# A new global order and engine choice for the 1444 operations of a fused long-convolution and gated-MLP kernel

## The chip, the cores and the metric

The kernel runs on one core of a Trainium2 chip. The core has five engines with a queue of instructions each: TensorE (PE in the profile; its weight loads are shown apart as PEld), VectorE (DVE), ScalarE (ACT), GpSimd (POOL) and SyncE (SP), whose queue here issues nearly all DMAs. The metric is the device time of one execution in microseconds; lower is better. A kernel's time is the median of several runs.

## What is computed

The inputs are 2048 tokens of 640 channels in bfloat16. Cut to what matters, the reference is this:

```python
mod = (silu(c) @ w_mod).reshape(1, 6, 1, 640)      # sa, ca, ga, sb, cb, gb
h = layernorm(q) * (1 + ca) + sa
# block A: a causal convolution of 4 taps, then one as long as the sequence
k_shift = sum(k_pad[:, t:t+S, :] * shift_k[:, 3-t] for t in range(4))
kv = k_shift * v
y = irfft(rfft(kv, 4096) * rfft(ssm_k, 4096))[:2048] + kv * ssm_D
x = q + ga * (h * y)
# block B: a gated MLP with a product over the sequence, Fh = 864
h = layernorm(x) * (1 + cb) + sb
z = gelu(h @ w_in)                                 # 2048 x 1728
z1, z2 = z[..., :864], layernorm(z[..., 864:])
g = w_sp @ z2 + b_sp[:, None]                      # w_sp is 2048 x 2048
out = x + gb * ((z1 * g) @ w_out)
```

## The kernel before

**How work is recorded and ordered.** The kernel does not issue instructions as it goes through its loops. Each step is recorded in a list, the class `Plan` (lines 119 to 154): `op(eng, kind, fn, ...)` stores which engines may do the step (`eng`, a string out of P, A, D, G, S for TensorE, ScalarE, VectorE, GpSimd, SyncE), a name (`kind`), the function that issues it, the tiles and parts of tiles that it reads and writes, and the tiles that it allocates. From these come its dependencies. There are 1444 steps; a step may be one instruction or many (the one called `taps` or `zz` issues up to ten and more matmuls). Then `Plan.run` (line 143) walks through the string `ORDER` (lines 47 to 114). A token of it such as `P1290` says: now issue step 1290, on TensorE. So this one string sets three things at once: the order in which each engine's queue is filled, the engine of every step that may go to more than one, and the order in which the tiles of a rotating pool are handed out. Between engines nothing but the dependencies sets the order. An engine does its queue strictly in order: where its next step has to wait, all behind it wait too.

**Steps 0 to 764, the convolution.** The 640 channels are cut into 5 slices of 128. For each slice u, `taps` multiplies K by diagonal weight matrices on TensorE (line 605), VectorE multiplies the result by V (`tv`, line 612), and the long convolution follows as three steps of matrix products: a first small transform (`s1`, copied out of PSUM by `s1c`), the forward transform with the tables M2 (`fwd`), for the filter and for the data, copies of the filter's half (`khc`, on ACT mostly), the complex product (`prod`, line 495, on VectorE), whose halves are summed by `csum` (line 505, GpSimd or VectorE), the inverse transform with the tables G2 (`inv`), casts of its result (`zc`, lines 278 and 514 on, ACT or VectorE), a transposing DMA (`zt`), and a last small transform (`y`). GpSimd and VectorE share the rest: the modulated h (`xn`, line 692; `ghm`, line 748, a multiplication by 1 + ca and an addition of sa), the gate and the residual (`ym`, `res`, line 808). The last slice has no time for a DMA, so TensorE transposes it (`zfl`, `zk`, `yl`, `yml`).

**The passage, steps 765 to 820 about.** The second layer norm of the first 512 tokens (`ag2`, `rstd2`, `nmr2`, `zx`), done in pieces as the last slice's columns come in; TensorE transposes each piece (`hfl`, line 971), VectorE and ACT modulate it (`hmod`, line 978; step 777 is one of those on VectorE). Step 1042 is one of four fillers (`fill`, lines 1062 to 1067): two matmuls of `ident` with itself, whose result nobody reads; it allocates a PSUM tile of the tag `s1`, which `hfl` uses as well.

**The MLP's first product, `zz` (line 1024).** 64 steps in 4 groups of 512 tokens, ten or so matmuls each step, GELU on ACT out of PSUM, statistics on VectorE (`stz`, line 1040), normalisation (`zn`, line 1052). Groups 1 to 3 are transposed by DMA (`turn`) and modulated by `hmod2`.

**The product over the sequence, steps 1045 to 1270.** The 16 row blocks of `w_sp` are taken in 8 pairs p = 0 to 7 (block p and block p + 8), and each pair's four products by the two halves of z2 are done with seven in Strassen's manner: `product(p, m)` (line 1115), m = 1 to 7, eight matmuls each. Their operands are sums of weight blocks, `ssum` (line 1096, VectorE or GpSimd, four for each pair), and sums of z2 blocks made once (`tsum`). The results are combined in SBUF by `keep`, `c11`, `partial`, `c22`, and by the closing pair `lsa` (line 1166) and `lsm` (line 1168, VectorE or GpSimd), which adds the bias and multiplies by z1. Two tiles u per pair (block p and block p + 8) then go through a transposing DMA, `turnu` (line 1173), into tiles uT. Steps 1137 and 1147, for example, are products of pair 1; the DMAs of its two blocks are 1142 and 1150.

**The projection, steps 1271 to 1443.** Pairs 0 and 7 are projected plainly (`pp`, line 1348). Pairs 1 to 6 use seven products again (`pq`, `piece`, line 1335): `usum` (line 1326, VectorE or GpSimd) makes four sums R of uT blocks for each pair, `vsum` makes those of the weights once; `ok`, `os`, `ox`, `oa` combine results, `pa` (line 1394) closes them with the residual, and a DMA writes each block of 128 tokens (`out`). Steps 1290 and 1292 are the first two `pq` of pair 1: 1290 needs the uT of block 1, 1292 the first sum R, which needs the uT of block 9. Step 1427 is the last `pq` of pair 6, 1430 the first `pp` of pair 7's first block. The weights of a pair are loaded by transposing DMAs (`ldwt`), 6 tiles in turn; there are 4 tiles uT.

**What sets the order in the old `ORDER`.** Per engine the string holds 407 steps for TensorE, 481 for VectorE, 272 for ScalarE, 189 for GpSimd and 95 for SyncE. In the spatial product TensorE runs, for each pair, products first and projections some six to eight steps behind: after product 1137 come six products and three `pp` before 1290, after 1147 three products and two `pq` before 1292.

## Time and profile before

| | |
|---|---|
| three runs | 305.51, 306.11, 307.37 us |
| median | 306.11 us |
| profiled execution, by its span | 303.8 us |
| DMA packets, bytes, mean rate | 117155, 41.57 MB, 137 GB/s |
| VectorE, busy | 260.4 us in 527 instructions |
| ScalarE, busy | 164.0 us in 299 instructions |
| GpSimd, busy | 186.8 us in 213 instructions |

The profile is one execution. Its span runs from the first instruction to the last; the runs' times hold what lies around it too. Busy time counts the instructions that compute; the issue of a DMA, a branch or a wait does not count. Matmuls overlap in their pipeline, so a TensorE that is busy throughout need not run at its peak, but it has no time in which it waits for anything. A row of the view by windows gives, for one stretch of time, each engine's busy time with the count of its instructions in brackets, the TensorE clock that the throttle granted as a share of full speed, the mean number of busy sixteenths of the DMA engines as a share, and the rate. A row of the view by groups gives the line of the code, the engine, the operation, output and input by the names of their tiles, and the sum and the mean duration of one; after the bar stands the idle time of the engine just before those instructions, and what ended it. In rows of the timeline the first column is the start in microseconds, the second the duration of all instructions of the row together.

### The profile page before, as it was taken

Reading aid. Unit: us, or ns where it says so; the run is one execution under the profiler, and the core shown is the slowest. Engines: PE = TensorE matmul, PEld = TensorE weight load, DVE = VectorE, ACT = ScalarE, POOL = GpSimd, SP = SyncE. Lnnn points to the kernel's source line nnn. Section 1 sums busy time; section 2 is a strip of 40 time slices with the busy share of each in tenths; the row PEclk is TensorE's granted clock in tenths of the full one; section 3 lists DMA queues with packets and bytes.
Section 4 is the critical chain, followed back from the end, with each engine's and each line's share of the span. In section 5 each row is a group of like instructions: output and inputs, shape, how many; then the busy total and the mean of one; then the engine's idle time right before and its main releaser. Section 6 shows DMA issues by size and latency. Waiting matters only on the chain.

```text
span 303.8 us, 7152 instructions
## 1 busy us (share of the span) xinstructions
PE 293.1 (96%) x2827; PEld 207.0 (68%) x2827; DVE 260.4 (86%) x527; ACT 164.0 (54%) x299; POOL 186.8 (61%) x213
## 2 busy tenths in 40 slices
PE   6899999999999999799999999999999999999996
PEld 2788999999989988645555555555555555665664
DVE  8899999999989999989595988988678798886794
ACT  5989999998888865446665779500111102111110
POOL 5463788839769997577537342099531863476771
PEclk9999999999999999869999999999999999999999
DMA  7999869792397978005997900057654446452433
GB/s 143 270 242 271 194 177 282 134 223 39 77 186 163 287 122 276 2 2 105 157 234 154 197 0 4 0 117 150 132 133 90 102 112 141 102 84 73 91 83 121
DMA packets 117155, 41.57 MB, mean 137 GB/s; under 512 B 102557, under 2 KB 117122, under 8 KB 117122
## 3 DMA queue, kind: packets, MB, share of 16 engines
q1 hardware_dynamic: 116968, 41.08, 62.0%
q8 instruction: 22, 0.36, 0.5%
q14 instruction: 11, 0.09, 0.1%
q10 hardware_dynamic: 154, 0.05, 0.1%
HBM read 16.60 MB, written 2.63 MB: 63 GB/s over the span
## 4 chain that ended last, share of the span: by engine, by line
PE 80%; DVE 8%; SPq 5%; DMA 3%; issue 2%; POOL 1%; ACT 0%; DVEq 0%; POOLq 0%
PE ps L1126 23%; PE pu L275 19%; PE pz L275 17%; PE po L1335 5%; PE sm L275 5%; PE s L275 4%; SPq L570 3%; DVE Tf L495 3%; PE po L1348 3%; DMA ZT<-in_A_v_dram 3%; PE pz L1126 2%; PE pu L1126 1%; DVE Z L616 1%; SPq L585 1%; DVE ot L1394 1%
## 5 line engine op out<-in xcount | busy, mean ns | idle before, releaser
L275 PEld LDWEIGHTS <-Z 128*128 128x128 bf16 x320 | 32.0, 100 | 28.8 <-issue 3.0
L275 PE MATMUL pu<-X,M 128*128 128x128 bf16 (+1 forms) x480 | 45.6, 237 | 0.9 <-DVE Tf L495 0.7
L509 POOL TENSOR_TENSOR W<-Tf 128x256 bf16<-128x256 f32 x42 | 30.7, 745 | 15.0 <-DVE Tf L495 9.0
L275 PEld LDWEIGHTS <-M 128*128 128x128 bf16 x480 | 36.7, 98 | 4.2 <-issue 1.6
L1126 PEld LDWEIGHTS <-S 128*128 128x128 bf16 x256 | 25.0, 98 | 20.8
L275 PE MATMUL pu<-big,Z 128*128 128x432 bf16 x160 | 34.6, 360 | 0.0
L278 ACT CAST X<-s 128x1024 bf16<-128x1024 f32 x32 | 32.7, 1021 | 3.3 <-PE s L275 3.2
L275 PE MATMUL pz<-big,Z 128*128 128x432 bf16 x160 | 33.0, 349 | 0.0
L495 DVE TENSOR_TENSOR Tf<-pu,KH 128x1024 f32<-128x1024 f32 x25 | 30.3, 1215 | 1.2 <-ACT Z L278 0.5
L1132 ACT COPY m<-ps 128x432 f32<-128x432 f32 x7 | 3.6, 521 | 49.8 <-PE ps L1126 41.0
L1126 PEld LDWEIGHTS <-wT 128*128 128x128 bf16 x192 | 18.8, 98 | 15.3
L278 ACT CAST Z<-pz 128x512 bf16<-128x512 f32 x40 | 23.5, 596 | 4.9 <-PE pz L275 4.7
L275 PEld LDWEIGHTS <-G 128*128 128x128 bf16 x330 | 24.6, 98 | 1.8 <-issue 0.4
L278 ACT CAST KH<-pu 128x512 bf16<-128x512 f32 x40 | 23.1, 592 | 3.8 <-PE pu L275 3.4
L1126 PE MATMUL ps<-X,wT 128*128 128x432 bf16 x112 | 22.7, 346 | 0.0
L1126 PE MATMUL ps<-X,S 128*128 128x432 bf16 x112 | 22.6, 346 | 0.0
L1040 DVE BATCH_NORM_STATS2 stz<-X 128x6 f32<-128x432 bf16 x32 | 18.1, 588 | 5.0 <-ACT X L1034 4.9
L1126 PE MATMUL ps<-T,S 128*128 128x432 bf16 x112 | 22.2, 346 | 0.0
L275 PE MATMUL sm<-dg,big 128*128 128x128 bf16 x320 | 20.7, 219 | 1.1 <-DVE Z L616 1.0
L275 PEld LDWEIGHTS <-big 128*128 128x128 bf16 x320 | 18.9, 98 | 2.0 <-issue 1.6
L495 DVE TENSOR_TENSOR T<-pu,KH 128x1024 bf16<-128x1024 f32 x15 | 18.2, 1215 | 1.9 <-PE pu L275 1.8
L275 PEld LDWEIGHTS <-X 128*128 128x128 bf16 x288 | 17.8, 98 | 2.2 <-POOL X L433 0.7
(223 smaller groups left out, 666.7 us busy)
## 6 DMA issues: line engine op xcount, KB each, us to landing
wm<-in_w_mod_dram SPq DMA_DIRECT2D x6, 800.0 KB, 4.9
xt<-in_A_q_dram SPq DMA_DIRECT2D x4, 640.0 KB, 5.6
out_dram<-ot SPq DMA_DIRECT2D x15, 160.0 KB, 1.9
big<-in_B_w_in_dram SPq DMA_DIRECT2D x2, 1080.0 KB, 7.8
X<-in_A_ssm_k_dram SPq DMA_DIRECT2D x4, 512.0 KB, 6.2
ZT<-in_A_v_dram SPq DMA_DIRECT2D x1, 1024.0 KB, 7.6
big<-in_A_v_dram SPq DMA_DIRECT2D x1, 1024.0 KB, 7.8
w_o<-in_B_w_out_dram SPq DMA_DIRECT2D x6, 160.0 KB, 3.5
```

What stands on the lines that cost most here:

```text
L275: nc.tensor.matmul(o, lhsT=w, rhs=x, start=start, stop=stop)
L278: (e.copy if e is nc.scalar else e.tensor_copy)(dst, src)
L495: e.tensor_tensor(T_[:], (tl[pu] if src is None else tl[src])[:, :, :, None, :].to_broadcast(shape), tl[KH][:, :, None, :, :].to_broadcast ...
L509: e.tensor_tensor(tl[W][:, :, o, :], T_[:, :, 0, o, :], T_[:, :, 1, 1 - o, :], op=ALU.add if o else ALU.subtract)
L570: e.dma_start_transpose(k_of(u)[:, KPAD + h * m:KPAD + (h + 1) * m], A_k[0, h * m:(h + 1) * m, u * DU:(u + 1) * DU])
L585: e.dma_start(v_of(0, ns.start, NT // n) if u0 == 0 else tl[name][:], v_nat[:, ns, ds])
L616: e.tensor_tensor(dst, tl[ps][:].rearrange("p n (c g) -> p n c g", g=8), v_of(u, i * SCH, SCH).rearrange("p n (c g) -> p n c g", g=8), op= ...
L1040: op("D", "stz", lambda e, i=i, n=n, fc=fc: e.bn_stats(out=stz[:, n, fc, :], in_=tl[z2][:, i, fc * FC:(fc + 1) * FC]), r=[(z2, (i, fc))], ...
L1126: nc.tensor.matmul(ps[:, :FC], lhsT=lhs[:, s_, :], rhs=rhs(s_), start=(s_ == 0 and not more), stop=(s_ == HT - 1), skip_group_check=more)
L1132: e.copy(part[p, m][:], part[p, BANK[m]][:, :FC])
L1335: nc.tensor.matmul(ps[:, :HS], lhsT=w(k), rhs=x(k), start=start and k == 0, stop=stop and k == n - 1, skip_group_check=True)
L1348: e.matmul(po[t, i][:, :hi - lo], lhsT=uTs[t][:fsz[ft], ft, :], rhs=T["w_o"][:fsz[ft], ft, lo:hi], start=(ft == 0), stop=(ft == NFT - 1))
```

## The change

Only the string `ORDER` is replaced: 68 lines by 70. No step is added, removed or altered; the same 1444 steps are issued, with the same dependencies and tile pools. What differs is the sequence, and the engine of about 130 steps that may go to more than one. By kind, old engine to new:

| steps | moved |
|---|---|
| `ghm` | 9 VectorE to GpSimd, 11 GpSimd to VectorE |
| `zc` | 5 ScalarE to VectorE |
| `zn` | 6 ScalarE to VectorE, 4 VectorE to ScalarE |
| `csum` | 6 VectorE to GpSimd, 5 GpSimd to VectorE |
| `ssum` | 6 GpSimd to VectorE, 2 VectorE to GpSimd |
| `usum` | 8 GpSimd to VectorE, 4 VectorE to GpSimd |
| `lsm` | 5 GpSimd to VectorE, 1 VectorE to GpSimd |
| the rest | single ones of `xn`, `zx`, `zk`, `s1c`, `hmod2`, `res`, `oa`, `c22`, `gbm`, tables |

VectorE's queue holds 502 steps after it (481 before), GpSimd's 173 (189), ScalarE's 267 (272); TensorE's 407 and SyncE's 95 stay, in another sequence. The lines of the string that hold the steps named above, old and new:

```diff
 ORDER = """
...
-D510 P519 A520 P529 S588 P688 P523 G511 A530 D512 D689 P690 P513 D691 A524 A514 D639 P692 D693 P724 P728 D725 A729 P694
...
-D767 G719 D768 D740 D706 G723 D741 G769 P751 D770 D742 D743 G771 A772 D700 P773 D699 D780 D745 P774 D775 D776 D777 G701
-A778 D721 D746 D781 A779 G676 G782 S598 D759 P1042 D748 D749 D704 D703 D702 G677 D783 D645 P793 D752 D760 D845 G784
...
-G1091 P1133 G1092 D1107 D1139 P1143 A1134 D1095 G1108 D1271 S1097 P1135 D1144 D1145 P1137 S1096 G1113 D1136 G1146 P1147
-S1088 P1158 P1283 D1140 P1281 D1141 D1111 S1100 G1110 S1142 D1282 D1148 P1151 D1109 P1153 D1149 A1152 D1284 P1155 S1099
-D1159 P1163 P1276 D1112 D1164 A1154 G1272 P1290 P1157 D1156 P1167 S1150 D1286 S1101 P1171 P1178 P1278 A1172 D1287 P1295
-D1274 D1160 S1285 D1165 A1291 D1273 D1115 D1296 D1161 D1114 D1277 P1175 P1173 D1168 D1288 A1174 P1292 P1183 P1302 P1177
...
-G1419 P1420 S1270 D1417 D1421 D1423 S1405 P1424 P1427 D1428 P1430 G1418 S1429 D1425 D1431 P1432 S1426 P1435 D1433 P1438
...
+P521 D522 P497 A498 P509 D510 P519 A520 G527 G528 P529 A530 S687 P688 D689 P523 G511 G512 D647 A524 P690 D691 D676
...
+D745 P758 D759 P1042 P751 G771 A772 P773 D775 D776 D780 D777 D781 G677 P774 A779 S765 A778 P796 P793 A797 D752 D746
...
+D1092 G1068 S1088 P1276 D1095 D1277 S1098 P1133 P1143 A1134 D1108 S1097 D1273 D1139 D1144 P1135 D1136 P1137 G1110
+D1140 D1141 P1278 D1279 S1096 P1281 D1145 D1111 P1147 D1148 G1146 D1149 P1151 S1142 P1290 A1291 D1282 P1153 D1272
+A1152 D1109 P1302 D1303 P1158 S1150 D1286 P1292 D1287 D1274 P1295 D1112 D1114 D1288 D1296 S1280 S1099 P1283 P1163
...
+G1418 G1419 P1420 D1421 D1425 S1426 P1430 P1427 D1428 P1432 S1429 D1431 D1433 S1434 P1435 P1441 D1436 S1437 D1442
...
 """
```

Read along one letter, the lines give one engine's queue. After product 1137 TensorE's now holds 1278, 1281, 1147, 1151 and then 1290; after 1147 it holds 1151, 1290, 1153, 1302, 1158 and then 1292. In the passage the filler 1042 stands ahead of 751, the last table product of the last slice; 511 and 512, the last two sums of the complex product, are both GpSimd's (512 was VectorE's). On SyncE's queue the first loads come in another sequence; then a load of modulation weights (573) goes ahead of a transposing load of K columns (31), another transposing load of K columns (33) ahead of a filter load (97), the two loads of `w_in` (765, 766) change places, and the first loads of the weights of the product over the sequence (1045 to 1052) come in another sequence around `turn` 919.

More of the change, by code (lines that the diff above doesn't have):

```diff
@@ L108 @@
[L108 to L111 removed]
+G5 D13 D0 D14 D18 A1 P7 D10 S2 P1044 G110 G109 D111 D112 G6 P8 P1043 A4 A16 G15 D17 A11 S83 S84 D113 D19 D90 D118 G89
@@ new lines @@
+P257 A258 A553 D65 P277 D278 G279 P100 A101 P315 A316 G105 P273 G559 D549 D270 D554 G555 P227 D228 P201 A202 S35 P66
+D67 G280 S579 P580 P283 D581 P591 A592 D274 P333 A334 D556 G565 S36 A564 D284 D569 D566 G570 G571 P271 A272 P72 A567
+P339 D73 P287 D288 A340 P293 D294 P70 P68 D71 D289 P329 A330 P383 A384 D572 P321 G74 G568 A322 P281 D282 P299 D300
+P337 S593 S594 G290 A560 D37 D600 P331 A338 A332 P285 A286 P303 D304 G604 P335 A336 P291 A292 D69 P323 A324 G295 P275
+D606 D623 D296 P317 A318 S595 D605 D607 P385 D660 D601 A386 P327 P297 A276 A328 G602 D603 D679 P341 D342 P389 A390
@@ new lines @@
+D631 P425 D426 A360 P435 P371 A372 P632 D633 P463 A464 P349 P634 P465 D723 A466 D436 D635 G683 S107 P481 A482 A350
+P421 P419 A420 P405 A406 P636 D422 D637 D638 D618 P483 A484 P397 A398 G617 P423 D424 D641 P477 A478 P487 P469 A488
+A470 P431 G427 G428 P429 A430 D663 D432 G437 G720 G438 P439 P441 D442 P485 A486 P451 S582 D452 P583 D640 P473 A474
+A440 A584 S666 D684 G620 P433 G659 P667 P471 A434 P479 G643 A472 D668 P669 D639 A480 G443 G444 P445 A446 D670 D642
+P489 D490 G453 G454 G717 G491 D645 P449 G682 A450 P671 D672 G492 P467 A468 P505 D506 P455 A456 P673 D674 G675 P475
@@ new lines @@
+G782 D644 D783 A784 D704 D749 D702 D750 G785 D747 P825 P787 A791 G648 S598 A794 D646 A826 P786 D845 D705 D748 D846
+D753 D844 D843 G847 D760 D764 D754 P827 A828 A792 D848 D849 G851 A852 G850 D788 S853 P823 P800 A801 P821 A822 D790
+A824 D789 P814 A815 G706 D619 D711 D649 D710 D653 D656 D678 D714 P829 A830 A140 D715 D652 D654 S599 S1046 P807 P831
+D707 D761 A832 S1045 P803 D651 A804 D757 P835 A836 P833 A857 A834 A808 D854 D855 P810 A811 D709 D713 P817 A818 G856
+D858 D655 P895 A896 D756 D911 D708 D755 D912 D650 D910 D909 G913 D805 P880 P893 A894 P859 A881 P901 A902 P862 D657
@@ new lines @@
+D879 D937 D886 D931 D865 P1012 D872 G903 D951 D952 D799 G837 D904 D941 D907 A992 G1057 G1059 D838 D1054 D1055 S1049
+D906 D934 D938 P994 A1013 A995 G1053 D945 G969 A840 P998 S1051 A999 D1000 P965 D1010 A966 P1015 A1016 D1017 D908 A842
+P963 A964 A841 P1001 P1019 A1020 A1002 P953 A954 P1031 D1007 A1032 D1011 D993 D970 D905 P961 A962 D839 A971 D1070
+D1003 G1056 P1023 D1014 D972 D1018 D1004 D996 D997 D1069 P1029 G1035 A1030 A1024 P1027 A974 P1021 A1022 D1036 P1025
+A1026 D1038 D1039 P1033 P1077 A1028 A1040 D1060 A1034 A1078 D973 D1037 D1071 D1072 D1075 D1073 D1074 D1058 P1079 A1080
@@ new lines @@
+D1169 G1298 D1305 P1178 P1171 D1294 D1297 D1301 S1162 P1314 A1315 A1172 S1170 D1310 D1311 S1101 G1313 D1116 D1179
+D1117 P1307 P1173 P1316 D1113 P1319 D1299 D1308 A1174 D1320 A1317 G1323 G1318 P1326 P1177 P1175 D1180 P1191 S1102
+S1285 D1119 D1176 D1181 S1182 S1306 D1322 D1120 P1183 D1184 A1192 P1195 D1327 D1321 P1187 D1185 G1186 D1312 P1338
+S1309 D1188 D1189 S1190 P1324 D1325 A1339 P1328 D1122 D1196 P1350 P1331 D1332 D1118 D1329 G1334 D1351 S1104 P1198
+D1199 D1335 D1337 S1330 S1333 D1336 P1203 D1204 P1193 A1194 G1205 G1206 P1343 D1344 P1340 P1348 A1341 D1121 P1197
@@ new lines @@
+D1200 D1201 S1103 P1352 P1207 P1211 P1213 A1214 S1202 D1347 D1342 D1208 P1362 D1209 S1210 D1125 G1345 D1349 D1123
+P1355 D1346 S1106 D1353 S1354 D1356 D1358 D1359 P1218 A1212 P1215 D1219 D1216 P1364 A1365 D1366 P1217 D1220 D1221
+P1367 A1363 D1368 G1360 P1372 G1361 P1223 D1369 D1224 D1225 G1370 P1374 P1376 D1375 P1227 D1373 D1228 G1226 G1229
+D1377 S1105 S1357 S1222 S1230 P1386 A1387 P1379 P1233 D1124 D1126 P1398 D1382 D1383 D1384 P1238 P1231 G1371 D1380
+D1399 D1127 P1388 A1389 D1390 D1128 D1130 A1234 A1232 D1239 P1391 P1396 G1385 P1400 D1392 G1395 P1243 D1244 D1129
```

85 lines of the change are left out of this document (29 added, 56 removed).

## The prediction

> **What bounds the kernel now.** I read the page first: its span, its busy shares and the row of the granted clock.
>
> ```profile
> span 303.8 us, 7152 instructions
> ...
> PE 293.1 (96%) x2827; PEld 207.0 (68%) x2827; DVE 260.4 (86%) x527; ACT 164.0 (54%) x299; POOL 186.8 (61%) x213
> ...
> PEclk9999999999999999869999999999999999999999
> ```
>
> TensorE (PE) is busy for 293.1 of 303.8 us, and the clock falls in two slices out of 40, the 17th and 18th (121.5 to 136.7 us). Then I cut the span by stage: the long convolution (0 to 119), the passage into the gated MLP (119 to 134), its first product (to 190.8), its spatial product and projection (to 290), the tail.
>
> ```profile
> core 0: us, PE busy (x) PEld busy (x) DVE busy (x) ACT busy (x) POOL busy (x), PEclk, DMA share, GB/s
> 0.00:25.00 25.00, 21.31 (x240) 16.79 (x241) 21.69 (x65) 20.79 (x46) 13.24 (x35) 1.00 1.09 216
> 25.00:60.00 35.00, 34.71 (x541) 32.86 (x541) 33.11 (x61) 34.03 (x64) 25.02 (x34) 1.00 0.89 217
> 60.00:90.00 30.00, 29.95 (x425) 28.04 (x424) 28.33 (x45) 26.23 (x40) 20.93 (x24) 1.00 0.66 122
> 90.00:119.00 29.00, 27.62 (x430) 25.41 (x427) 27.74 (x38) 22.41 (x38) 26.30 (x31) 1.00 0.81 210
> 119.00:134.00 15.00, 12.71 (x219) 9.16 (x220) 14.22 (x43) 5.66 (x10) 10.15 (x12) 0.77 0.14 48
> 134.00:190.80 56.80, 56.80 (x321) 30.70 (x319) 45.93 (x133) 39.63 (x74) 28.02 (x31) 1.00 0.58 114
> 190.80:290.00 99.20, 99.20 (x582) 56.67 (x581) 80.00 (x129) 14.39 (x30) 57.22 (x44) 1.00 0.49 103
> 290.00:303.80 13.80, 10.83 (x81) 7.34 (x79) 9.34 (x21) 0.84 (x2) 5.90 (x7) 1.00 0.39 106
> ```
>
> From 134 to 290 PE is never idle and its clock is 1.00: no order can win there, it can only lose. All of PE's idle time is 10.7 us: 3.7 before 25 (while the DMA share is 1.09, so transfers set the pace), 1.7 from 25 to 119, 2.3 in the passage, 3.0 in the tail. In the convolution VectorE (DVE) is idle for only 1.9 + 1.7 + 1.3 = 4.8 us of 94, so there it is nearly a bound itself, and from 25 to 60 ScalarE (ACT) too. The passage shows the one thing that is plainly out of place:
>
> ```profile
> 126.72 2.26 POOL L808 TENSOR_TENSOR xt<-xt,gh 128x512 bf16<-128x512 bf16 x2
> 128.54 0.72 DVE L753 TENSOR_TENSOR gh<-gh,gsa_bf 128x512 bf16<-128x512 bf16 x1
> 128.69 1.03 PE L275 MATMUL s<-ident 128*128 128x512 bf16 x2 [0.78 <-DVE Z L985]
> 129.51 3.81 PE L275 MATMUL pu<-big,Z 128*128 128x432 bf16 x10
> ```
>
> The clock filler `P1042` (third row) waits until the modulations have freed its PSUM tile, then stands 0.8 us (128.69 to 129.51) in front of the MLP's first product, whose matmuls take 0.38 us each (3.81 / 10) under the fallen clock.
>
> **The change part by part.** It is one list, so I take it by stage. Durations are those of this one execution, so the sum is made against its span of 303.8 us; the median of the runs shown, 306.1, lies 2.3 above it, and I add that at the end.
>
> ```profile
> L278 DVE CAST X<-pu 128x512 bf16<-128x512 f32 x3 | 2.0, 681 | 0.0
> L278 DVE COPY X<-sm 128x1024 bf16<-128x1024 bf16 x6 | 4.0, 668 | 0.1
> L699 DVE TENSOR_SCALAR gh<-xt,mv,rstd 128x640 bf16<-128x640 bf16 x2 | 1.4, 688 | 0.0
> L753 DVE TENSOR_TENSOR gh<-gh,gca_bf 128x512 bf16<-128x512 bf16 x11 | 4.4, 437 | 0.0
> L753 DVE TENSOR_TENSOR gh<-gh,gsa_bf 128x512 bf16<-128x512 bf16 x10 | 5.1, 510 | 0.0
> L509 DVE TENSOR_TENSOR W<-Tf 128x256 bf16<-128x256 f32 x8 | 3.4, 433 | 0.2
> L509 POOL TENSOR_TENSOR W<-Tf 128x256 bf16<-128x256 f32 x42 | 30.7, 745 | 15.0 <-DVE Tf L495 9.0 <-PE pz L275 5.0 <-PE s L275 1.0
> L856 DVE TENSOR_TENSOR gh<-gh,pz 128x512 bf16<-128x512 bf16 x2 | 1.2, 625 | 0.0
> ```
>
> *Convolution, VectorE's load up to the last modulation before the MLP (`D777`).* New on VectorE ahead of it: five `zc` casts from ACT (5 x 0.68 = +3.4), two `xn` (+1.4), three `ghm` (3 x 0.47 = +1.4), one `yml` moved ahead (+0.6). Gone: two `zk` (-1.3), one `s1c` (-0.7), one `csum` (-0.4). Some ten small table operations change engine (`diag`, `f1m`, `f1g`, `turns`, `ident`, `mneg`); together I put them at -0.5 to +0.5 and count nothing, because VectorE is idle for 3.3 us in the first 25 us. Sum +4.4, less what was double: by my list of both orders 189 operations become 195, +3.7 us. It lies on the path: VectorE's idle time is its only cover. Against it stands what a better order saves: idle 4.8 us and waits at the port it shares with GpSimd (POOL). The second passage row shows such a wait: 0.72 us beside POOL's `xt`, against 0.44 in the group. If all idle time went and some 2 us of port waits too (an estimate: 0.28 us at each of the seven or eight such operations), the term is 3.7 - 6.8 = -3; if none goes, +3.7. I take half of the saving: +0.3.
>
> *Which engine relieves which.* `zc` on VectorE frees ACT 0.6 us each, but ACT gets `zk`, `s1c`, `xn` back, and in the window where it is nearly full (34.03 of 35) its sum hardly moves: 0.
>
> *DMA order.* On SP's queue the load of the v columns stays behind the same set of transfers, so the first 25 us stay; K columns for the third slice go one 800 KB weight load later, and one filter load goes behind a transposing load. I count 0: both are first read some 5 us after they would land, by the pace above.
>
> *The passage.* The filler goes ahead of the last table product, into idle time: -0.8, at most the 1.03 of its row. Both halves of the last complex sum (`511`, `512`) now go to POOL, one behind the other: 2 x 0.745 instead of one beside the other, +0.5 on the path to the last inverse transform. Together -0.3; in the clock nothing is counted.
>
> *First product, 134 to 190.8.* VectorE's and ACT's sums before it ends hardly move (45.93 and 39.63 of 56.8 now). PE covers: 0.
>
> *Spatial product and projection.* Here the load moves most: POOL's list from 49 operations to 32, VectorE's from 134 to 147.
>
> ```profile
> L1101 DVE TENSOR_TENSOR S<-wT 128x1024 bf16<-128x1024 bf16 x13 | 12.7, 976 | 2.2 <-DMA wT<-in_B_w_sp_dram 2.2
> L1101 POOL TENSOR_TENSOR S<-wT 128x1024 bf16<-128x1024 bf16 x3 | 7.2, 2394 | 0.0
> L1326 DVE TENSOR_TENSOR R<-uT 128x384 bf16<-128x384 bf16 x8 | 3.7, 466 | 1.5 <-DMA uT<-u 1.5
> L1326 POOL TENSOR_TENSOR R<-uT 128x384 bf16<-128x384 bf16 x4 | 3.7, 930 | 2.6 <-DMA uT<-u 2.6
> L1166 DVE SCALAR_TENSOR_TENSOR c<-ps,bcol,s 128x432 f32<-128x432 f32 x14 | 9.3, 662 | 3.5 <-PE ps L1126 2.4 <-POOL u L1168 0.9
> L1168 DVE TENSOR_TENSOR u<-c,M 128x432 bf16<-128x432 f32 x5 | 4.3, 868 | 0.1
> ```
>
> Four more `ssum` (+3.9), four `usum` (+1.9), four `lsm` (4 x 0.87 = +3.5) and some singles: about +10 us, so VectorE's 80.0 of 99.2 become 90. That still fits under PE. What changes is slack. PE now takes each pair's projections much earlier, and those wait for a chain: product, `lsa` (0.66), `lsm` (0.87), the transposing DMA, for some `usum` (0.47).
>
> ```profile
> L1173 SPq DMA_TRANSPOSE uT<-u x16: 1220/1222/1353, 206.0 to 294.4; - x16
> ...
> DMA to landing us min/median/max: 2.9/2.9/3.7
> ```
>
> ```profile
> 227.62 0.95 PE po L1348 x7
> 234.32 7.30 PE ps L1126 x40
> 250.33 0.54 PE po L1335 x4
> ```
>
> A product of 8 matmuls is 1.46 us (7.30 / 5), a `pp` 0.95, a `pq` 0.54. Between pair 1's product `P1137` and its first projection `P1290` stood six products and three `pp`, 11.6 us; in the new list two and two, 4.8. The chain needs 0.66 + 0.87 + 2.9 = 4.4, and some tenths for four hand-overs. Likewise between `P1147` and `P1292`: three products and two `pq`, 5.5, against 4.4 + 0.5. I find such edges, with under 1 us to spare, about twelve times (two for each of six pairs); before, those edges had 5 to 17 us. Each costs nothing when the chain runs free, 0.9 us when one more operation (0.87) stands ahead on VectorE or the DMA takes its 3.7. Bounds 0 and 12 x 0.9 = 11; a late pair also delays the next pair's products, so they don't add up: half the edges late by 0.3, about +1.5.
>
> *Tail.* `P1430` goes before `P1427`, which waited for a closing sum on VectorE: at most one `pp`'s cover, -0.2.
>
> Sum: +0.3 - 0.3 + 1.5 - 0.2 = +1.3 us on 303.8, 305.1; with 2.3, 307.4, a change of +0.4%. A gain or loss under 1% (about 3 us) can't be told from no change in this kernel.
>
> **A rule weighed.** The Trainium skill, SBUF — State Buffer, "Who interferes with whom", says that a VectorE operation with two SBUF inputs contends with a GpSimd operation that reads SBUF, and that whoever issued first holds the pair for its whole instruction. The row of 0.72 us agrees. By that rule alone each operation taken from POOL removes a wait, and the convolution's term would go to its lower end, -3. The skill's TensorE: Matmul & The Clock Gate, Part 1, says the clock returns after about 3.4 us of busy window; by it a filler moved ahead of the gap may leave the clock to fall as before. The trace agrees in size: the ten slow matmuls of the fourth passage row last 3.81 us.
>
> **The rivals.**
> *Faster.* The port waits and idle time go (-3), the filler's 0.8 is won and the two halves of `csum` hide (0), the chains run free (0), and the clock falls for half as long: ten matmuls at 0.38 instead of 0.18 lose 2.0 us now, so -1. Together -4.8 - 0.2 = -5: 301. For it: VectorE is the bound and 6.8 us of it are idle or waiting. Against: it gets 3.7 us more to do.
> *Slower.* The twelve edges decide. From one operation's wait (0.9 us) at half of them, less the tail's and the filler's gain of 1, the loss passes 3 us; with 0.5 at all twelve it is 6, and 311. For it: slack of 0.0 to 1.0 by rows, and a VectorE at 90 of 99. Against: the longest landing of 16 was 3.7, the usual one 2.9.
> *It does nothing.* PE covers all of it, 306.1; it is within my forecast.
>
> **How the numbers follow.** About no change (307) has 0.38; the faster case 0.32; the slower 0.30. The range takes 301 in and reaches to 311.5, which leaves a tenth out on each side; the likeliest case's own range is 303 to 309. By the same cases: faster 0.32, same 0.38, slower 0.30.
>
> **What would show it.** Right: in the new trace PE has idle time between 190.8 and 290, released by SP's `uT` or by VectorE's `u` and `R`, where it had none; VectorE's busy time before the first product is longer by 2 to 4 us or its idle time smaller; the filler runs before the piecewise flips and the first product follows them directly; POOL's busy time is smaller by some 25 us. Wrong: the first product starts before 126 us, so that the convolution's port waits were worth more than I take; or PE stays gap-free from 134 to the tail; or waits at the weights of the next pair, whose loads moved behind the turns.

## The result, and the profile after

The changed kernel takes 313.62 us (median of 4 runs, 313.0 to 314.01) against 305.93 us before (4 runs): a ratio of 1.0249, 95% interval 1.0215 to 1.0283. It is slower, by 7.7 us; 307.0 was forecast, and 313.6 lies outside the range of 301 to 311.5. The profiled execution has a span of 312.2 us against 303.8.

The page of the changed kernel; its line numbers are two higher than before, since the string is two lines longer:

```profile
span 312.2 us, 7134 instructions
...
PE 294.2 (94%) x2827; PEld 206.5 (66%) x2827; DVE 272.6 (87%) x547; ACT 160.0 (51%) x291; POOL 165.8 (53%) x198
...
PEclk9999999999999999979999999999999999999999
```

TensorE does the same work in 8.4 us more, VectorE is busy 12.2 us longer (272.6 against 260.4), GpSimd 21 us less. To see where the 8.4 us arise, the span has to be cut where each kernel passes from one stage to the next, not at equal times. The two views by windows, of the kernel before and of the changed one, are cut at the end of the last inverse transform, the start of the MLP's first product and its end, the end of the first pair's seven products, and the end of the last pair's:

```profile
0.00:118.40 118.40, 113.35 (x1628) 102.98 (x1629) 110.27 (x204) 102.89 (x184) 84.89 (x121) 1.00 0.85 190
118.40:129.50 11.10, 8.45 (x214) 7.34 (x211) 10.32 (x30) 4.87 (x8) 6.79 (x8) 0.89 0.24 87
129.50:190.80 61.30, 61.30 (x333) 32.63 (x332) 50.43 (x148) 40.98 (x76) 31.98 (x35) 0.96 0.54 106
190.80:201.00 10.20, 10.20 (x57) 5.47 (x56) 9.11 (x12) 3.08 (x6) 2.89 (x3) 1.00 0.00 1
201.00:292.90 91.90, 91.90 (x543) 52.89 (x542) 73.63 (x123) 11.32 (x24) 56.82 (x45) 1.00 0.52 111
292.90:303.80 10.90, 7.93 (x64) 5.66 (x62) 6.61 (x14) 0.84 (x2) 3.40 (x4) 1.00 0.48 132
```

```profile
0.00:125.00 125.00, 114.74 (x1628) 103.27 (x1629) 117.07 (x208) 99.26 (x177) 87.77 (x121) 1.00 0.83 179
125.00:134.90 9.90, 8.22 (x214) 7.41 (x210) 9.59 (x27) 3.81 (x7) 6.01 (x7) 0.91 0.30 109
134.90:196.30 61.40, 60.74 (x331) 31.87 (x332) 53.92 (x142) 42.31 (x78) 33.23 (x36) 0.99 0.52 105
196.30:209.60 13.30, 10.67 (x57) 5.38 (x56) 11.51 (x23) 2.46 (x4) 3.61 (x4) 1.00 0.00 1
209.60:302.00 92.40, 92.40 (x547) 53.19 (x545) 74.51 (x137) 11.74 (x25) 31.68 (x29) 1.00 0.54 112
302.00:312.20 10.20, 7.38 (x61) 5.37 (x59) 5.97 (x13) 0.43 (x1) 3.48 (x4) 1.00 0.47 125
```

The second number of a row is the stage's length. Convolution 118.4 to 125.0: +6.6. Passage 11.1 to 9.9: -1.2. First product: +0.1. The first pair's seven products 10.2 to 13.3: +3.1, of which TensorE's idle time is 2.6. All that follows to the last pair's end: +0.5, with TensorE busy throughout in both; the new list does four more matmuls there (547 against 543) and as much less behind. Tail: -0.7. These are the 8.4 us. In the convolution TensorE's row count is the same (1628 matmuls), and its idle time, length less busy time, goes from 5.1 to 10.3 us. VectorE's idle time hardly moves (8.1 and 7.9), its busy time grows by 6.8.

What TensorE waits for, in the convolution and then in all that follows, by the view of waits of the changed kernel:

```profile
PE sm L633 <- DVE Z L618: 1.4, 1, 1.4
PE pz L277 <- DVE W L511: 1.1, 1, 1.1
PE sm L277 <- DMA wm<-in_w_mod_dram: 0.9, 1, 0.9
PE s L277 <- POOL X L435: 0.7, 1, 0.7
```

```profile
PE pu L1128 <- DVE T L1113: 1.7, 1, 1.7
PE pz L1128 <- DVE c L1157: 0.8, 1, 0.8
```

The numbers are total, times, longest. In the convolution there is no single large wait but a dozen, on different producers; the longest that the kernel before does not have is 1.4 us (one of 2.3 us at the start, for the first load, has its like of 2.6 there). After it there are only two that count, both in the first pair (0.5 us more lie in the first product): on VectorE's sums of z2 (`T`, line 1113) and on a closing sum that frees a PSUM bank (`c`, line 1157). No projection of pairs 1 to 6 waits for anything.

Two of the convolution's waits, in the timeline of TensorE and of VectorE and GpSimd:

```profile
44.97 0.60 PE L277 MATMUL pz<-W,G 128*128 128x256 bf16 x6 [1.08 <-DVE W L511]
```

```profile
43.07 1.84 DVE L511 TENSOR_TENSOR W<-Tf 128x256 bf16<-128x256 f32 x2
```

```profile
43.04 1.60 POOL L511 TENSOR_TENSOR W<-Tf 128x256 bf16<-128x256 f32 x2
...
8.92 2.83 POOL L378 TENSOR_SCALAR T<-KH,mstep 128x256 f32<-128x256 f32 x2 [2.69 <-ACT M L383]
...
15.71 0.26 POOL L435 TENSOR_TENSOR X<-X,D_col 128x16 bf16<-128x16 bf16 x1
```

At 43 us each of the two engines does two sums of the same kind (`csum`), side by side, and VectorE takes 0.92 us for each where the row quoted in the prediction had 0.43. That agrees with the Trainium skill, SBUF — State Buffer, "Who interferes with whom", by which an operation with two SBUF inputs on VectorE contends with a GpSimd operation that reads SBUF. At 8.9 us a table step that VectorE did before in 1.06 us (step 124; the one ahead of it took 0.61) takes GpSimd 2.83, and the small addition at 15.71, for which TensorE waits, stands behind it and five more.

### The profile page after: what moved, and what is told of

Same layout as the page of the kernel before. It is cut to its first block, busy times and chain, and to the rows that moved or that the text cites. A ratio compares the mean times of both kernels' runs of the same rounds, so it can differ in the third digit from the quotient of the medians.

```text
span 312.2 us, 7134 instructions
## 1 busy us (share of the span) xinstructions
PE 294.2 (94%) x2827; PEld 206.5 (66%) x2827; DVE 272.6 (87%) x547; ACT 160.0 (51%) x291; POOL 165.8 (53%) x198
## 3 DMA queue, kind: packets, MB, share of 16 engines
q1 hardware_dynamic: 116968, 41.08, 61.3%
## 4 chain that ended last, share of the span: by engine, by line
PE 35%; DVE 12%; POOL 3%; DMA 3%; issue 1%; POOLq 0%; DVEq 0%
PE ps L1128 23%; PE po L1337 7%; DMA Z<-Z 3%; DVE stz L1042 3%; PE po L1350 2%; DVE X L1059 2%; PE pz L277 1%; DVE st L816 1%; DVE T L1113 1%; POOL rstdz L221 1%; PE pu L277 1%; POOL Z L1013 1%; DVE w_o L1205 1%; DVE Z L1013 1%; POOL Z L961 1%
## 5 line engine op out<-in xcount | busy, mean ns | idle before, releaser
L277 PEld LDWEIGHTS <-Z 128*128 128x128 bf16 x320 | 31.2, 98 | 29.3 <-POOL Z L1013 1.3
L511 POOL TENSOR_TENSOR W<-Tf 128x256 bf16<-128x256 f32 x43 | 32.0, 763 | 24.0 <-DVE Tf L497 18.5
L280 ACT CAST X<-s 128x1024 bf16<-128x1024 f32 x30 | 30.6, 1020 | 4.8 <-PE s L277 4.5
L277 PE MATMUL pu<-big,Z 128*128 128x432 bf16 x160 | 32.3, 346 | 0.1
L1402 ACT COPY O<-po 128x320 f32<-128x320 f32 x12 | 5.0, 425 | 47.6 <-PE po L1337 47.6
L280 ACT CAST KH<-pu 128x512 bf16<-128x512 f32 x40 | 23.8, 602 | 5.0 <-PE pu L277 4.5
L280 ACT CAST Z<-pz 128x512 bf16<-128x512 f32 x35 | 20.3, 597 | 7.9 <-PE pz L277 7.9
L1042 DVE BATCH_NORM_STATS2 stz<-X 128x6 f32<-128x432 bf16 x32 | 17.9, 583 | 1.7 <-ACT X L1036 1.7
```

Of the source, the lines that this page charges most:

```text
L277: nc.tensor.matmul(o, lhsT=w, rhs=x, start=start, stop=stop)
L280: (e.copy if e is nc.scalar else e.tensor_copy)(dst, src)
L511: e.tensor_tensor(tl[W][:, :, o, :], T_[:, :, 0, o, :], T_[:, :, 1, 1 - o, :], op=ALU.add if o else ALU.subtract)
L1042: op("D", "stz", lambda e, i=i, n=n, fc=fc: e.bn_stats(out=stz[:, n, fc, :], in_=tl[z2][:, i, fc * FC:(fc + 1) * FC]), r=[(z2, (i, fc))], ...
L1402: late("A", "ok", lambda e: e.copy(rows(i), po[p, b][:, :HS]), r=[o[b]], w=[O[i]], new=[(O[i], "O%d" % i)])
```

## The experiments

The stages of the runs, as their traces have them. "First pair" is its seven products, "pairs 1 to 7" all from there to the last product, with the projections in between; the tail ends here with the issue of the last output's DMA, 2.1 us before the span does. The first pair, the pairs behind it and the tail repeat to 0.2 us where nothing in them or ahead of them on VectorE was changed, and the first product moves with the clock (last section). A convolution's length is good to no more than 1.5 us: in the six kernels that have it as before it ends between 118.4 and 119.9. Against their mean of 119.1 the changed kernel loses 5.9 us there, not 6.6. The expectations count the first pair up to a later cut (17.9 us in the kernel before, 21.6 in the changed); up to it the new list holds seven matmuls of a projection as well, so 0.6 of that difference of 3.7 is other work.

| run | convolution | passage | first product | first pair | pairs 1 to 7 | tail | median us | ratio to before |
|---|---|---|---|---|---|---|---|---|
| before | 118.4 | 11.1 | 61.3 | 10.2 | 91.9 | 8.9 | 305.93 | |
| changed | 125.0 | 9.9 | 61.4 | 13.3 | 92.4 | 8.2 | 313.62 | 1.0249 (1.0215 to 1.0283) |
| new_conv | 125.0 | 9.9 | 63.4 | 10.2 | 91.9 | 8.9 | 313.80 | 1.0273 (1.0230 to 1.0316) |
| new_mlp | 118.9 | 11.3 | 61.9 | 12.9 | 92.4 | 8.2 | 309.74 | 1.0143 (1.0091 to 1.0196) |
| new_mix | 118.9 | 11.3 | 62.4 | 10.5 | 92.4 | 8.2 | 306.89 | 1.0043 (1.0027 to 1.0060) |
| order_only_conv | 140.7 | 9.8 | 64.1 | 10.2 | 91.9 | 8.9 | 330.10 | 1.0788 (1.0742 to 1.0833) |
| engines_only_conv | 135.3 | 11.8 | 60.4 | 10.2 | 91.9 | 8.9 | 322.87 | 1.0563 (1.0539 to 1.0586) |
| before_zc_dve | 120.5 | 11.3 | 60.8 | 10.2 | 91.9 | 8.9 | 307.17 | 1.0044 (1.0023 to 1.0065) |
| after_zc_act | 125.2 | 9.9 | 61.3 | 13.1 | 92.4 | 8.2 | 313.60 | 1.0265 (1.0224 to 1.0307) |
| after_ghm_dve | 124.3 | 9.8 | 60.7 | 13.3 | 92.4 | 8.2 | 312.52 | 1.0233 (1.0211 to 1.0255) |
| after_ghm_pool | 125.3 | 9.8 | 61.1 | 13.3 | 92.4 | 8.2 | 313.78 | 1.0271 (1.0252 to 1.0290) |
| after_points | 125.0 | 9.5 | 61.1 | 13.3 | 92.4 | 8.2 | 313.18 | 1.0236 (1.0185 to 1.0288) |
| after_points_late | 124.9 | 9.8 | 61.0 | 13.3 | 92.4 | 8.2 | 313.62 | 1.0249 (1.0209 to 1.0289) |
| before_points | 123.4 | 11.3 | 60.7 | 10.2 | 91.9 | 8.9 | 310.38 | 1.0142 (1.0105 to 1.0179) |
| after_start_old | 124.3 | 9.9 | 61.4 | 13.2 | 92.4 | 8.2 | 313.00 | 1.0235 (1.0212 to 1.0257) |
| before_start_new | 122.4 | 11.3 | 60.6 | 10.2 | 91.9 | 8.9 | 308.83 | 1.0095 (1.0069 to 1.0121) |
| after_gbm | 124.8 | 9.9 | 60.9 | 12.8 | 92.4 | 8.2 | 312.63 | 1.0207 (1.0167 to 1.0247) |
| before_fill | 119.9 | 9.8 | 60.3 | 10.2 | 91.9 | 8.9 | 304.24 | 0.9947 (0.9926 to 0.9968) |
| fill8 | 119.3 | 9.8 | 60.3 | 10.2 | 91.9 | 8.9 | 304.52 | 0.9960 (0.9943 to 0.9977) |
| fill8_tail | 119.1 | 9.8 | 60.2 | 10.2 | 91.9 | 9.8 | 305.31 | 1.0001 (0.9979 to 1.0023) |

**Which stages carry the loss.** Two kernels divide the list at step 793, the first step of the MLP's first product; a third takes only the steps from 1045 on from the new list. Where two lists are joined, each keeps its own sequence, and they are interleaved by the times of the traces.

```diff
 new_conv: steps 0 to 792 and the fillers
-ORDER of before
+ORDER of the change
 new_mlp: steps 793 on
-ORDER of before
+ORDER of the change
 new_mix: steps 1045 on
-ORDER of before
+ORDER of the change
```

> Steps 0 to 792 and the fillers (convolution and passage) in the new order and on the new engines, all later steps as before. Theory (the loss is made where VectorE is the bound): the stages add up, the convolution's +6.6 us and the passage's -1.2 of the two traces stay, so 305.9 + 5.4 = about 311.3 us (ratio 1.018). Rival (the stages hide each other: what is lost ahead of the first product is taken from slack behind it, or the loss needs the new MLP order as well): 306 to 308 us.

> The reverse: steps 793 on (first product, spatial product, projection) in the new order and on the new engines, convolution and passage as before. Theory: +3.2 us, all of it in the first pair's products, where TensorE waits for VectorE's sums of z2 and for a bank (1.9 + 1.0 us idle in the trace of the changed kernel), less 0.4 in the tail: about 308.7 us (ratio 1.009), and TensorE without a gap between pair 1 and the tail. Rival (the short edges between products and projections, as predicted): gaps released by the transposed u or by R, spread over pairs 1 to 6.

> Only the steps from 1045 on (spatial product and projection) in the new order and on the new engines; convolution, passage and first product as before. Theory (the first pair's wait of 3.3 us comes from the first product's order, which finishes the last group's statistics 4.1 us later; the new projection order costs nothing): the first pair in 17.9 us as before, the tail 0.4 to 0.7 us shorter, 304.7 us. Rival 1 (the wait comes from VectorE's order inside the spatial product): first pair 20 to 21 us, 308 to 309 us. Rival 2 (the short edges, as predicted): gaps from pair 1 on, 307 us and more.

The stages come along with their part of the list, the convolution's 125.0 and most of the first pair's loss, and nothing is taken back behind. The times add up less well: the two halves lose 8.4 and 4.4 us by the medians, the whole list 7.7. Most of the surplus lies in the first product, which is 2.1 and 0.6 us longer in these two than before. new_conv is 2.5 us above the theory's 311.3, and the row of its first product holds most of that:

```profile
134.90:198.30 63.40, 61.83 (x331) 32.47 (x332) 52.32 (x153) 43.61 (x80) 28.23 (x32) 0.95 0.53 102
```

It takes 63.4 us where the kernel before took 61.3. TensorE idles for 1.57 us in it, 1.1 of them in one wait for a piece of the layer norm (`Z`, line 957), and the clock stays low longer than before (last section). In new_mlp and new_mix TensorE has no gap from pair 1 to the tail, so the short edges are out. The first pair's loss divides: 0.3 us come with the new list of the spatial product alone (10.5), another 2.4 with that of the first product (12.9), and 0.4 more in the changed kernel.

**Engines or order?** Of the steps that change engine (150 in all, and not the 130 or so named with the change) 77 lie in the convolution and the passage, steps 0 to 792. Two kernels have there one of the two, the new order or the new engines, without the other.

```diff
 order_only_conv: steps 0 to 792 in the new sequence
-the engine letters of the change
+the engine letters of before
 engines_only_conv: steps 0 to 792 in the sequence of before
-the engine letters of before
+the engine letters of the change
```

> Convolution and passage (steps 0 to 792) in the new order, but each step on its old engine; all later steps as before. Known ends: old order with old engines 305.4 us, new order with new engines 313.8 us. Theory E (the choice of engines makes the loss: up to the end of the second slice 13.25 us of steps came to VectorE and 8.82 left it): VectorE is back at its old load, so 306 to 308 us. Theory O (the sequence makes it: steps such as the early first-norm statistics and eight gate multiplications stand ahead of products that TensorE waits for): 311 to 314 us.

> The reverse: the kernel before with the new engine for every step of 0 to 792, its sequence unchanged. Theory E: the load moves to VectorE whatever the sequence, so 311 to 314 us, with the last inverse transform at 124 to 126 us. Theory O: 306 to 308 us. Both near 310: each order fits its own engines, and neither part is the cause by itself.

Neither theory holds: the order alone costs 24.6 us, the engines alone 17.4, both together 8.4. Their rows from 0 to the last inverse transform:

```profile
0.00:140.70 140.70, 120.70 (x1627) 107.03 (x1628) 115.70 (x203) 101.71 (x182) 88.17 (x123) 0.98 0.73 160
```

```profile
0.00:135.30 135.30, 117.93 (x1628) 105.33 (x1629) 116.88 (x208) 101.62 (x179) 85.90 (x120) 0.99 0.75 168
```

VectorE's busy time is about that of the changed kernel in both (115.70 and 116.88 against 117.07), in the first even with each step on its old engine, where the kernel before had 110.27: its `csum` take 0.60 us there instead of 0.43. But it idles for 25.0 and 18.4 us where the two matched lists let it idle for 8. (The lower clock of the rows, 0.98 and 0.99, can make 3.4 and 1.7 us of the two lengths.) The sequence and the engines are one design; a price for "the steps that change engine" has no meaning without the sequence.

**Is it VectorE's load?** The five casts `zc` were moved back, and, the other way, moved alone in the kernel before. Then the multiplications `ghm` were cut down, once VectorE's and once GpSimd's.

```diff
 after_zc_act
-D208 ... D212 ... D228 ... D282 ... D424
+A208 ... A212 ... A228 ... A282 ... A424
 before_zc_dve: the reverse, in the list of before
 after_ghm_dve, after_ghm_pool (VectorE's or GpSimd's alone)
-e.tensor_tensor(gvu, gvu, vec[:, None, d0:d0 + du]..., op=o)
+e.tensor_tensor(gvu[:, :, :16], gvu[:, :, :16], vec[:, None, d0:d0 + 16]..., op=o)
```

> The changed kernel with its five casts zc that went from ScalarE to VectorE put back on ScalarE, at the same places of the list. Theory (VectorE's load sets the convolution's time one to one): 5 x 0.68 = 3.4 us back, 313.6 - 3.4 = 310.2 us. Rival (the new sequence makes the waits, whatever engine does the casts): 313 to 314 us, and the same stage length up to the last inverse transform, 125 us.

> The kernel before with only those same five casts moved from ScalarE to VectorE, at their old places of the list. Theory (VectorE's load): +3.4 us, 309.3 us (ratio 1.011), the last inverse transform ending at about 121.8 instead of 118.4. Rival (VectorE's idle 8.1 us in the convolution take them up): 306 to 307 us.

> The changed kernel; each of the 23 gate multiplications and additions (ghm) that run on VectorE, all after 68 us, works on 16 of its 128 columns instead of all. Left out is that part of h; what the others do is unchanged. Theory L (in the changed order VectorE's load sets the convolution's pace): some 0.25 to 0.3 us of each 0.43 go, 6 to 7 us of VectorE, and most of it, 4 to 6 us, comes off the end of the last inverse transform (125.0 us): about 308 to 309.5 us. Rival (the sequence's waits between engines set the pace, and VectorE only waits in another place, as with the five casts): under 1.5 us gained, 312 to 314 us.

> The changed kernel; each of the 17 ghm that run on GpSimd works on 16 of its 128 columns instead of all; VectorE's work is untouched. Theory P (GpSimd's long instructions hold the shared port, and 5.6 us of VectorE's convolution from 60 to 125 us are such waits): 2 to 3 us gained, with VectorE's ghm and csum closer to 0.4 us each: 310.5 to 311.5 us. Rival 1 (GpSimd's own queue is what the sums csum wait in): 4 us and more. Rival 2 (neither): under 1 us, 313 to 314 us.

The casts back on ScalarE gain nothing (1.0265 against the changed kernel's 1.0249); moved alone they cost 1.8 us by the medians, half of the theory's 3.4. Cutting GpSimd's multiplications gains nothing (1.0271). Cutting VectorE's gains 0.7 us in the convolution, less than its scatter, and 1.1 us by the medians (0.5 by the ratios), where the theory wanted 4 to 6. VectorE's busy time up to the last modulation before the MLP did fall, from 127.35 to 122.89:

```profile
0.00:134.70 134.70, 123.95 (x1838) 111.53 (x1838) 122.89 (x237) 103.50 (x185) 91.55 (x127) 0.98 0.78 174
```

So VectorE's load is not paid one to one. My expectation also missed a limit that the profile had: all these `ghm` run after 64 us, and from 60 to 119 us TensorE idles for only 1.7 us in the changed kernel (0.8 and 0.9 in the rows further down). No more than that could be won there.

**Single waits.** Each of TensorE's waits names a step that stands on the wrong engine or behind another. Five of them were mended in the changed kernel, three of the five in a second one, and six such moves were made alone in the kernel before.

```diff
 after_points
-G124 G20 ... S91 G96
+G124 G20 S26 S27 S91 G96
-D240
+A240
-D231 D232 ... G562 ... G215 ... G216
+D231 G232 ... G215 ... G216 G562
-A101 ... G512
+D101 ... D512
 after_points_late: without the first two
 before_points
-D124 A240 G231 G232 D101 D512
+G124 D240 D231 D232 A101 G512
```

> The changed kernel with five places mended where its trace shows TensorE waiting for one step: the sum addD 96 goes ahead of three table steps on GpSimd, copy 240 back to ScalarE, of the two complex sums 231 and 232 the second to GpSimd (and xn 562 behind its sums there), copy 101 back to VectorE, the last complex sum 512 back to VectorE. Theory W (TensorE's waits at single places make the loss): 0.9 + 0.8 + 0.7 + 1.0 + 0.4 = 3.8 us, so about 310 us, and the last inverse transform ends at about 121.5 instead of 125.0. Rival (some engine is full over the whole stretch; a wait that is mended comes back at the next place): under 1 us, 313 us.

> Only the last three of the five places (232 to GpSimd, 101 to VectorE, 512 to VectorE). Theory W: 0.7 + 1.0 + 0.4 = 2.1 us, 311.5 us. Rival: under 0.7 us.

> The kernel before, its sequence unchanged, with six steps on their new engine: table step 124 to GpSimd, copy 240 to VectorE, sums 231 and 232 to VectorE, copy 101 to ScalarE, sum 512 to GpSimd. Theory W: each makes its own wait, 2 to 4 us in all, 307.5 to 309.5 us. Rival: 305 to 306.5 us, since the engines that take them have room.

In the kernel before, the moves do cost: 4.2 us by the medians, of which 3.5 lie ahead of the first forward transform (18.6 us against 15.1), where table step 124 goes to GpSimd. VectorE's timeline there shows how one step holds up a queue: it stands still for 3.04 us until GpSimd has done the step, which takes it 2.28 us there, and the multiplication by V that TensorE needs (line 616) stands behind it. The clock fell in the same stretch, to 0.50 from 14.9 to 18.3 us, so not all of the 3.5 us need be the wait.

```profile
13.16 0.70 DVE L378 SCALAR_TENSOR_TENSOR T<-T,KH 128x512 f32<-128x512 f32 x1 [3.04 <-POOL T L376]
...
13.99 0.68 DVE L616 TENSOR_TENSOR Z<-sm,big 128x512 bf16<-128x512 f32 x1
```

In the changed kernel, mending the places gains nothing: the last inverse transform ends at 125.0 and 124.9. In after_points' view of waits another step has taken their place, the small addition ahead of the third slice's transform, which now stands behind the sum that was moved to GpSimd:

```profile
PE s L275 <- POOL X L433: 1.3, 1, 1.3
```

So this mended wait came back at the next place, and the theory that the sum of the single waits is the loss falls for the changed kernel.

**Where in the convolution?** The two kernels exchange the 150 steps that ran in the first 25 us of the kernel before.

```diff
 after_start_old: the 150 steps of the start
-ORDER of the change
+ORDER of before
 before_start_new
-ORDER of before
+ORDER of the change
```

> The changed kernel with the 150 steps that ran in the first 25 us (tables, first loads, first slice's first transform) in the old order and on their old engines; 18 of them change engine by it. Theory S (the start makes its own share): 2 us gained, about 311.5 us, the last inverse transform at about 123. Rival (the part from 25 us on sets the time whatever the start does): no gain, 313 us or more.

> The reverse, the kernel before with only those 150 steps in the new order and on their new engines. Theory S: 2 us lost, 307.5 to 308 us. Rival: under 0.7 us lost.

The changed kernel by the windows of the prediction, then after_start_old, then before_start_new:

```profile
0.00:25.00 25.00, 19.37 (x211) 14.83 (x212) 20.73 (x58) 19.09 (x39) 18.25 (x38) 1.00 1.08 228
25.00:60.00 35.00, 32.66 (x506) 30.30 (x504) 33.13 (x61) 31.01 (x62) 18.50 (x26) 1.00 0.85 195
60.00:90.00 30.00, 29.20 (x406) 27.05 (x404) 29.05 (x45) 24.64 (x38) 23.03 (x26) 1.00 0.59 107
90.00:119.00 29.00, 28.13 (x436) 26.19 (x434) 28.48 (x40) 21.59 (x36) 23.50 (x27) 1.00 0.80 176
```

```profile
0.00:25.00 25.00, 21.43 (x237) 17.25 (x238) 21.69 (x65) 20.43 (x44) 14.79 (x36) 1.00 1.05 223
25.00:60.00 35.00, 32.59 (x494) 30.10 (x492) 32.99 (x59) 31.16 (x60) 19.24 (x27) 1.00 0.82 199
60.00:90.00 30.00, 28.79 (x401) 26.69 (x400) 29.05 (x45) 24.22 (x36) 22.38 (x25) 1.00 0.60 112
```

```profile
0.00:25.00 25.00, 20.15 (x202) 15.66 (x203) 20.75 (x56) 18.71 (x40) 16.38 (x37) 1.00 1.04 226
25.00:60.00 35.00, 33.07 (x522) 31.23 (x520) 31.05 (x61) 32.50 (x64) 21.48 (x29) 1.00 0.71 184
```

In the changed kernel TensorE's busy time falls behind the old by 1.9 us up to 25, by 2.1 from 25 to 60 and by 0.8 from 60 to 90 (21.31, 34.71 and 29.95 in the prediction's rows). With the old start the first deficit is gone (21.43), yet the second stays (32.59), the third grows (28.79), and the median is 313.0 (1.0235), no measurable gain. In the kernel before, the new start costs 3.1 us (1.0095). So the new start is bad by itself, and the part behind it is bad whatever the start does. What in the steps from 25 to 60 us sets that pace was not found: the runs exclude VectorE's casts alone, the five waits alone and, from 64 us on, both engines' `ghm`. The new sequence of the loads was not tried alone; TensorE waits 0.9 us for a load of modulation weights and 0.5 us for a transposed slice (`ZT`) in the changed kernel, which it does not in the kernel before.

**The first pair.** By the view of the chain of waits the time from the last group's modulation to the first pair's products goes through VectorE's queue, with GpSimd's reciprocal roots (`rstdz`) in between, and only then TensorE takes over:

```profile
174.22 0.41 DVE Z L1013
...
181.74 1.35 DVE nmrz L1051
183.09 2.01 DVE w_o L1205 x2
...
200.82 2.02 DVE T L1113 x2
...
208.01 1.62 PE pz L1128 x8
```

The last group's last statistics end 0.7 us before the first product is over (195.6 against 196.3); before it was 4.7 us (186.1 against 190.8), in new_conv 4.7, in new_mix 4.1, in new_mlp 1.1. It goes with the first product's list. One suspect, two weight multiplications on VectorE at 183 us, was moved.

```diff
 after_gbm
-D1054 ... D1055 ... G1035
+G1054 G1055 G1035
```

> The changed kernel with two weight multiplications (gbm 1054, 1055) taken from VectorE at 183 us, where they stand ahead of the last group's statistics and take 2.1 us beside GpSimd's, to GpSimd at 190 us, where it idles for 5.8 us. Theory (from 174 to 208 us the first pair waits for VectorE's queue, one step behind the other): the first pair's stretch falls from 21.6 to 19.5 us, 311.5 us. Rival (the statistics are late because ScalarE and TensorE deliver them late): no change, 313.5 us.

The first pair fell by 0.5 us, not 2.1, and the statistics still end 1.2 us before the product does. The two steps make a sixth of the 3.1 us; the rest was not taken apart further.

**The filler, and a version that beats both.** Filler 1042 was moved alone; then it got 8 matmuls; then the new tail was added.

```diff
 before_fill
-P751 ... P774 ... P1042
+P1042 P751 ... P774
 fill8
-FILLS = (4, 2, 2, 2, )
+FILLS = (4, 8, 2, 2, )
-P751 ... P774 ... P1042
+P751 P1042 ... P774
 fill8_tail: the same, and steps 1412 on
-ORDER of before
+ORDER of the change
```

> The kernel before with one step moved: filler 1042 ahead of the last table product 751 of the last slice, as in the new order. Theory (the passage's gain of 1.2 us between the two traces is the filler's place): the time from the last inverse transform to the first product of the MLP falls from 11.1 to about 10.0 us and the fallen clock lasts some 3 us instead of 6.8, together -1 to -2 us: 303.4 to 304.4 us. Rival (TensorE waits for the norm of the last slice anyway): no change.

> The kernel before with filler 1042 directly behind table product 751 and with 8 matmuls instead of 2, so that TensorE idles for about 0.5 instead of 2.2 us ahead of the first transposes. In the runs so far the clock stayed down for whole multiples of 3.41 us (3.4, 6.8, 10.2), and each multiple went with about 1.0 us of the first product. Theory (idle time ahead of the transposes sets off the fall): no fall or one that is over before the first product: 303 us, about 1 us under the kernel with the filler of 2 in front of 751 (304.2 us). Rival (the 1.4 us around the transposes set it off as well): one window of 3.4 us stays, 304 us.

> The same with the steps from 1412 on (last projections) in the new order and on the new engines, where the tail was 0.7 us shorter in every run that had them (8.17 against 8.87 us). Theory (the tail's gain is independent of all ahead of it): 0.5 to 0.7 us under the run beside it, 302.3 us. Rival (it hangs on the projections ahead of the tail): no change against it.

The filler's place is worth 1.3 us of the passage (11.1 to 9.8) and 1.0 of the first product, and before_fill is the fastest kernel of the study: 0.9947 (0.9926 to 0.9968). Eight matmuls keep the clock at 1.00 through the passage and the product, and gain nothing more. The first product of before_fill, then of fill8:

```profile
129.65:189.94 60.29, 60.20 (x331) 32.15 (x332) 51.45 (x151) 41.82 (x78) 32.76 (x36) 0.98 0.54 107
```

```profile
129.10:189.40 60.30, 59.61 (x332) 31.91 (x333) 51.59 (x151) 41.63 (x78) 32.73 (x36) 1.00 0.54 107
```

TensorE is faster in the second (59.61 us busy), and waits for the difference: at the start of the product others set the pace. The new tail, 0.7 us shorter with the projections of the change ahead of it, is 0.9 us longer behind the old ones, and fill8_tail takes 0.8 us more than fill8 by the medians.

## Why the prediction was wrong, step by step

- **The convolution, forecast at +0.3, is +6.6.** This is the step that failed: "I take half of the saving", set against a new load of +3.7. The load came out at twice that and the saving did not come.
  - The load. Up to the same last modulation VectorE is busy for 127.35 us against 119.68, +7.7. About 5 of it are the steps that moved, at the durations they had before or have now where they are new: the prediction wrote "one `s1c` (-0.7)", but three casts of 0.68 us went and two of 1.22 came. More than 2 are operations that became longer, the `csum` left on VectorE above all (0.43 to 0.67 us). The ten small table operations do sum to nothing on VectorE, as assumed; one of them went to GpSimd and is the step of 2.83 us.
  - The saving. The port waits were to shrink by half of 2 us; by the longer `csum` and the rows at 43 us they grew. The 2 us also rested on a wrong pair: the row of 0.72 is an addition of sa, whose group has a mean of 0.51; the 0.44 is the multiplication's. VectorE's idle time was to shrink by half of 4.8 us; from 25 us on it fell to 3.7, but ahead of that it grew by 1.0, and over the stage it is 7.9 against 8.1.
  - The bound. The upper end of the term, +3.7, was none, because it bounded one engine's load, while TensorE waits for whatever step it finds unfinished. Taking load from VectorE again gained nothing (after_zc_act) or less than the scatter (after_ghm_dve), but of these steps only the casts run ahead of 64 us. Which steps from 25 to 60 us make the loss stays open.

```profile
L511 DVE TENSOR_TENSOR W<-Tf 128x256 bf16<-128x256 f32 x7 | 4.6, 674 | 0.0
L280 DVE CAST X<-s 128x1024 bf16<-128x1024 f32 x2 | 2.4, 1220 | 1.1 <-PE s L277 1.1
```

- **The passage, forecast at -0.3, is -1.2.** The direction and the place are right; before_fill shows that the filler alone makes it. The size was too small because only the filler's own 0.8 us was counted. Its wait of 0.78 us for the modulations, in the third passage row, went with it: from the first transposes to the first product it is 2.7 us in the kernel before (126.8 to 129.5) and 1.4 in before_fill (128.3 to 129.7). The 0.5 for `csum` 511 and 512 belongs ahead of the last inverse transform, to the convolution, and giving 512 back to VectorE (after_points_late, with two other moves) gained nothing measurable there.
- **The DMA order, forecast at 0,** was not tried alone; TensorE's two new waits for transfers, 0.9 and 0.5 us, are what the trace shows against it.
- **The first product, forecast at 0, is +0.1**, but "PE covers" holds only to its last step. The work it hands on comes 4 us later, and TensorE pays 3.1 us in the first pair, a term that the sum put at nothing. The prediction looked at VectorE's sum in that window (45.93 of 56.8) and not at when the last group's statistics end.
- **The twelve short edges, forecast at +1.5, are 0.** Pairs 1 to 7 take 92.4 us in every kernel with the new projections and 91.9 with the old, without a gap in either. VectorE has more room there than the prediction gave it: its busy time from the first product's end to the last pair's grew from 82.7 to 86.0 us, not by 10, because its operations became shorter while GpSimd's busy time fell from 59.7 to 35.3. An `ssum` takes 0.84 us instead of 1.06 in that stretch, and the `lsm` that was priced at 0.87 takes 0.61 (row below). That the one follows from the other was not tried alone. The rival that ended on the slower side was right in sign and wrong in place. I had let it carry the range's upper end.

```profile
L1170 DVE TENSOR_TENSOR u<-c,M 128x432 bf16<-128x432 f32 x5 | 3.0, 605 | 0.1
```

- **The tail, forecast at -0.2, is -0.7**, but 0.5 of it is work done earlier, the +0.5 of the pairs ahead of it. The two together are -0.2.
- **What was to show it.** TensorE does idle between 190.8 and 290, but released by `T` and `c`, in the first pair alone; the filler runs ahead of the flips and the first product follows them; GpSimd's busy time is 21 us smaller (25 forecast). VectorE's up to the first product is 6.1 us longer (2 to 4 forecast). The difference of the median to the span, put at 2.3, was 1.4 here; a run's time is about 1.8 us above its own span, and the 2.3 compared two runs.

## What to carry to other kernels

Where TensorE and VectorE are both nearly full, an order and a choice of engines are one design: taking one without the other cost 17 to 25 us here, both together 8, and single repairs gave back next to nothing. Before such a change is priced, look for each stage not at the sum of the engine that is full but at when the last input of the next stage is finished, since a stage whose own length does not change can still hand its delay on. A step that moves into a gap that the profile shows plainly, such as the filler, can be tried alone, and it was the one part of this change that gained time by itself.
